# Last 64 channels mixed in four 64x64 tiles, weights asked for later, a wider output ring and a new hand-written order, in a convolution and token-mixing kernel

## The chip, the cores and the metric

The kernel runs on one core of a Trainium2 chip. A core has TensorE (PE in the profile; its weight loads are shown apart as PEld), VectorE (DVE), ScalarE (ACT), GpSimd (POOL) and SyncE (SP), which run their own instruction streams and meet through semaphores, and 16 DMA engines that move data between the chip's main memory and the core's own memory (SBUF). Matmul results land in PSUM, which has 8 banks of 128 partitions x 512 float32 values. The metric is device time in microseconds (us); lower is better. Here it is the median of the runs of one kernel.

## The reference

The input x has shape (8, 4224, 192): 8 batches, 4224 tokens, 192 channels.

1. A causal convolution over 7 tokens. The channels form 8 heads of 24; each head has its own 7 taps, which are a softmax over a row of `weight` (8, 7). `y[s] = sum_k w[h, k] * x[s - 6 + k]`.
2. A linear token mixing with `w_q` and `w_k` (192, 64): `W_tok = (y w_q)(y w_k)^T / 8`, `mixed = W_tok y`, with no softmax.
3. `out = relu(mixed) w_out`, with `w_out` (192, 192).

As step 2 has no softmax, it can be computed as `mixed = (y w_q) (w_k^T (y^T y)) / 8`. The 4224 x 4224 matrix is never formed; what is formed for each batch is the 192 x 192 Gram matrix `G = y^T y` and the 64 x 192 matrix `M = w_k^T G / 8`.

## The kernel before

**Work of one batch.** The tokens stand on 128 partitions in 33 chunks of 128. A batch goes through these kinds of operations (the names are those of the program):

- *load* (POOL's queue): x arrives as bfloat16 in one of `NX` places of `XW`, in two DMAs (batch 0 in four).
- *conv* and *conv_other* (PE, L575): one pair for each head, each four 64x64 matmuls against a banded matrix; two PSUM banks. *y* (ACT or DVE, L607) copies the result to `Y` as bfloat16. Batch 0 is cut into three pieces of chunks, so it has 24 pairs and 24 evacuations.
- *yt* (DVE, L622): four operations that transpose `Y` in 32x32 blocks; *wq* (PE, L640): 48 matmuls of 512 columns in 32x64 tiles give `y w_q` transposed in four banks; *wqt* (L657) evacuates it into `WQT` in two halves, one for tokens 0 to 2047 and one for tokens 2176 to 4223, on partitions 0 to 63 and 64 to 127. The middle chunk has a path of its own (*tr_mid*, *ytl*, *wq_mid*, *wqt_mid*).
- *gram* (PE, L708): six operations that accumulate G; *g*, *turn*, *gt*, *m*, *ms*: G is evacuated, partly transposed, multiplied with w_k and scaled into `MSB` (128 channels) and `MBD` (the last 64 channels, block-diagonal).
- *mix_lo* (PE, L801) and *mix_hi* (PE, L809 or L813): mixed and transposed for 4 x 512 tokens in each half and for the middle chunk; *rt* and *rh* (L827, L828) evacuate them through relu into `RT`. mix_lo covers channels 0 to 127 in two banks, mix_hi the last 64 channels in one bank.
- *fin* and *fin_other* (PE, L859, L876): products with `w_out`; *out* (L894) copies two banks into one of `NOUT` places of `OUT`; *store* (SP's queue, L906; the middle chunk's is L907) writes a place to main memory once both *out* operations that fill it are done. A later *out* that uses the same place waits until that store has landed.

**Order.** `PLAN`, a list written out in the source, gives one order for all 921 operations: an entry is a number, a letter and PSUM banks. The letter chooses the engine (A is ACT, D is DVE, G is POOL, S is SP) or, on PE, the shape of the tiles in which the matmuls are issued: F is the full 128x128 array, C is 128x64 tiles (two at once), R is 64x128 (two at once), Q is 64x64 (four at once), W is 32x64. Each engine executes its own entries strictly in the order of the list; so do the two DMA queues, POOL's with the loads and SP's with the weights and stores. `Program.place` puts in front of each operation the semaphore waits that its inputs, its PSUM banks and its buffers need; a wait holds up everything behind it on the same engine.

**Places of the rings** are in one line: `NX, NYT, NRT, NOUT = 6, 1, 4, 7` (x, transposed y, relu results, outputs).

**Order around the change.** "store 3.1" below is the first store of batch 3 in SP's order, "out 3.9" the ninth *out* of batch 3 in the plan. Decoded from `PLAN`:

- SP's stores, in order: 0.1 0.2 0.3 1.1 0.4 1.2 0.5 1.3 1.4 1.5 2.1 2.2 3.1 3.2 2.3 2.4 2.5 3.3 4.1 3.4 4.2 3.5 and so on. Store 3.1 needs out 3.3 and out 3.5; store 2.3 needs out 2.6 and 2.7; store 2.5 needs out 2.1 and 2.5. Out 3.9 uses the place of store 2.5.
- DVE between *wq* of batch 0 and *wq* of batch 1: wqt, g, y, y, gt, ms, cast, ms, cast, ms, y, yt, rt, yt, yt, rh, yt (and then rt, out, y, out, y).
- PE around *wq* of batch 0: gram (4), wq, gram (2), eight conv pairs of batch 1 with turn and m among them.
- PE's 479 operations change tile shape 128 times. mix_hi for 512 tokens is issued 8 times as F (one matmul) and 24 times as C (two matmuls).

**Start.** The taps become banded matrices through a chain of small DVE, ACT and PE operations; four weights (w_k; w_q in two layouts; w_out) are asked for on SP's queue as soon as the taps' weights have landed, in 12 DMAs. PE executes a few matmuls on zeros (*run_up*) first.

Of the kernel before, what the change touches and what calls it, by code (L numbers as in the profile page):

```python
# [22 lines left out]
119Q 104Q 114D 120A 662G 105D 111A 134C2 138C3 52A 135D 130D 143C 559G 140C 128D 142C 560G 129D 131W64 661G 141C
132A 133D 139C 159Q0 144D 156Q6 160Q 157Q 153Q4 161A 174Q2 158D 175Q 154Q 171Q0 176A 155D 172Q 162Q6 173A 145C2
163Q 146D 168Q4 164A 147C3 165Q0 148D 169Q 53D 166Q 149D 170A 47D 150D 763G 167D 136C2 212R6 137A 201R4 234R2
177D 203A 188C0 764G 235C1 214D 193C 213C4 202C5 190C 204A 178D 192C 237A 189C 236A 179D 224C6 191C 215A 226D
241R2 194A 180D 267Q4 223R6 242R 225D 268Q 243A 208R0 209F 269A 270Q2 210D 255Q6 271Q 256Q 272A 219R4 257D 227R0
220R 228R 221A 261Q2 229D 273Q6 262Q 274Q 263A 216R4 275D 230R0 217R 231R 181W26 232A 218A 195C0 183D 196A 264Q4
182A 197F1 184F0 265Q 198D 276Q6 266D 199A 258Q2 200A 277Q 259Q 278A 304F1 260D 205R4 185A 238R6 306A 206R 303R2
207A 239R 290C0 240D 305A 293C 211S 281D 233S 186C1 245R4 314R6 222S 247A 310R2 316A 187D 325R4 279D 311R 291C  # L30
327A 280D 326C1 315C6 246C7 295C 317A 248D 292C 282D 312A 294C 286C4 328A 249R5 307R6 287D 296A 250R 251D 308R
347R2 366Q0 349D 363Q4 309D 367Q 372Q2 364Q 368A 373Q 365D 313S 357Q6 374A 297C0 252S 337C1 298D 378Q4 339A 358Q
369Q2 379Q 359A 360Q0 380D 361Q 370Q 375Q6 362A 371D 376Q 462Q4 377A 463Q 336R0 464D 283W26 338A 340R4 284A 285D
341F 299F0 342A 321R2 300D 329R6 301D 382D 302A 322R 318R4 343R0 323A 330F 344F 331D 348C2 345A 428F3 319F 350D
332R6 381D 320A 405R0 351R2 333F 407A 352F 439C4 392C5 441D 334A 395C 353D 397C 430D 354S 288C0 406C1 244S 393C
383D 408A 324S 388C4 438R6 389A 335S 427R2 440D 417C1 346S 429A 396C 394C 419A 289D 384D 471Q6 398A 477Q2 472Q
478Q 480Q0 473D 468Q4 479A 481Q 469Q 482D 470A 434R6 416R2 435F 418D 385W40 436A 420R6 387A 386D 412R2 421R 413R
422A 465Q0 414D 474Q4 466Q 475Q 467A 459Q6 476D 570Q2 460Q 571Q 461A 409R0 399F4 410F 400D 572A 483D 401F5 431R6
402A 411A 442R2 403D 432R 404D 443R 433A 445R4 415S 449R0 444D 446F 451A 423R6 447A 529R0 519F2 530F3 531A 424F
532D 508F4 494C5 425A 521D 450C0 497C 486D 452A 426S 510A 576Q2 579Q6 561Q0 577Q 580Q 562Q 578D 581A 498C 496C  # L40
563A 484D 490C4 453R2 518R6 507R0 520D 454R 390C3 499C 491A 495C 455A 509A 541C4 391D 485D 564Q6 573Q2 565Q 574Q
500D 533R0 575A 566D 534F 535A 582Q2 543D 663Q6 583Q 664Q 567Q4 584A 684Q0 665D 568Q 685Q 569A 514R2 686D 522R6
515R 511R4 516A 523R 512R 524D 540R0 513A 596C2 501C3 542A 525R6 502D 551R4 526F 553D 503F3 487W40 504D 505A
527A 506A 528S 547R6 489A 488D 517S 552C3 597C 448S 554A 548R 585D 456S 536R0 549A 544R4 437S 537R 587D 545R
538A 631R6 599C 546D 633A 539S 601C 632C3 492C0 586D 634A 493D 555R1 620R4 609R6 622A 556R 621C3 588D 600C 592C0
611A 598C 557D 593D 610C4 602D 643C5 612D 589W06 645A 623A 774Q4 590A 591D 669Q2 775Q 670Q 671A 642R0 776D 768Q6
644A 603C2 594C3 604D 769Q 595D 681Q4 765Q2 770A 682Q 766Q 683D 638R0 767A 624R6 639R 613R4 640A 625R 614R 649R2
616R0 650R 617R 615A 626D 651A 646R4 618D 635R6 647R 653R2 636R 648D 655A 619S 783Q0 637A 678Q2 550S 784Q 679Q
785A 675Q4 680D 786Q6 676Q 787Q 677A 666Q0 788D 654C2 667Q 656A 605F3 668A 672Q4 606D 771Q6 607D 673Q 772Q 608A
780Q0 674A 773D 777Q2 781Q 778Q 782A 723F4 779D 657R5 627R6 725A 722R0 658R 628R 688D 711R2 659A 629A 734C4  # L50
698C5 689D 724A 630S 699C 558S 687D 712C6 694C7 713A 703C 652S 745C0 700C 714D 641S 695A 701C 690D 747A 702C
736A 744R2 704A 733R6 746D 715R0 735A 729R4 716R 730F 717D 691W26 731D 726R0 693A 692D 740R4 727R 741R 728A
718R6 792D 751R2 742A 732S 748R0 719R 752R 749R 720A 705C4 800C5 706D 750D 753A 696C4 721S 707C6 756C7 802C 708A
758D 697A 754S 790D 709A 755R2 737R0 710A 660S 757A 813R6 759R4 791D 738R 760R 846R2 761A 804C 815A 789D 762S
825C4 801C 848A 739D 814C6 805C 847C7 816A 827D 803C 743S 849A 824R2 806D 820R0 826D 835R6 817R4 837A 821F 818F
822D 850R2 819A 828R6 851R 853R0 823S 852A 829R 807C4 858C5 854R 808A 860D 831R2 830D 855A 809F4 832F 836F5 856S
833A 793W06 838D 810D 834S 811D 812A 842R2 794A 795D 839R4 843R 840R 844A 841D 865R0 866C6 867A 878C7 868D 796C2
845S 877R4 797A 869R0 879A 857R2 870F 859D 880D 873R2 871A 861R6 798C4 874F 799D 872S 862R 901R0 875D 881R4 903A
902F7 882F 904D 876S 890C2 863A 914C3 883D 892A 864S 905R0 889R6 906R 891D 884S 909R4 907A 910F 908S 911A 885R0
916D 913R6 897R2 915D 886R 912S 898R 887A 893R4 917R6 899D 894F 918F 888S 919A 895D 900S 920S 896S  # L60
# [121 lines left out]
def bass_lightweight_conv__then__hypermixer_token_mlp_kernel(  # L182
# [8 lines left out]
    B, S, D = x.shape  # L191
    H, KC = weight.shape
    DH = moe_w_q.shape[1]
# [23 lines left out]
    NX, NYT, NRT, NOUT = 6, 1, 4, 7  # L217
# [242 lines left out]


# [33 lines left out]
    def gen_weight(name, pairs):  # L495
        def emit(e, op):
            return [(e.dma_start(d, s), 16) for d, s in pairs]

        return add(
            "S", emit, needs=[load_w], dma=(name, semaphore(f"s_{name}"), 16 * len(pairs)), kind="weights"  # L500
        )

    def split(t, n, cols):
        return [
            (WLO[:, cols], bass.AP(t, 0, [[n, LO], [1, n]])),
            *((WHI[p : p + HI, cols], bass.AP(t, LO * n, [[n, HI], [1, n]])) for p in (0, HI)),
        ]
# [5 lines left out]
            (WQ6F[32 * i : 32 * i + 32, :, :], bass.AP(wq_t, 0, [[2 * DH, 32], [64 * DH, 3], [1, 2 * DH]]))  # L513
            for i in range(NBLK)
        ],
    )
    load_t = gen_weight("wt", [split(wq_t, DH, QS)[i] for i in (0, 2)])
# [267 lines left out]
    def gen_mix(b, j, evm):  # L785
# [11 lines left out]
        def mix_lo(e, op):  # L797
            last = None
            for i in range(2):
                p = slice(64 * i, 64 * i + DH)  # L800
                last = e.matmul(  # L801
                    bank(op.bank[0] + i)[:, 0:n], MSB[p, mb, :], WQT[p, wqb, q0 : q0 + n], start=True, stop=True
                )
            return last

        def mix_hi(e, op):
            ps = bank(op.bank[0])
            if op.letter == "F":
                return e.matmul(ps[:, 0:n], MBD[:, mb, :], WQT[:, wqb, q0 : q0 + n], start=True, stop=True)  # L809
            last = None  # L810
            for i in range(2):
                to = ps[64 * i : 64 * i + HI, 0:n] if whole else ps[0:HI, n * i : n * i + n]
                last = e.matmul(  # L813
                    to, MBD[:, mb, 64 * i : 64 * i + HI], WQT[:, wqb, q0 : q0 + n],
                    start=whole or i == 0, stop=whole or i == 1, skip_group_check=True,
                )
            return last

        ml = add("R", mix_lo, needs=[*evm, *evq], after=free, banks=(2,), kind="mix_lo", batch=b)
        mh = add("FC" if whole else "C", mix_hi, needs=[*evm, *evq], after=free, banks=(1,), kind="mix_hi", batch=b)  # L820
# [3 lines left out]
        def relu(dst, src):  # L824
# [8 lines left out]
        hi_to = RT[:, slot, 2, 0:n] if whole else RT[0:64, slot, 2, 0 : 2 * n]  # L833
# [4 lines left out]
        )  # L838
        rh = add(
            "AD",  # L840
            relu(hi_to, lambda: bank(mh.bank[0])[:, 0:n] if whole else bank(mh.bank[0])[0:64, 0 : 2 * n]),
            needs=free, drains=(mh, 0), kind="rh", batch=b,
        )

# [147 lines left out]
```

## Time and profile before

| | |
|---|---|
| three timed runs | 169.04, 167.09, 168.16 us; median 168.16 us |
| profiled execution | 168.92 us; span of its instructions 167.2 us |
| mean granted TensorE clock in it | 0.928 of full |
| busy share of the span | PE 86%, DVE 71%, ACT 68%, POOL 13% |
| moved by DMA | read 26.49 MB, written 25.95 MB |

In the page, line 2 of the profile cuts the span into 40 slices of 4.18 us; a digit is the busy share of a slice in tenths, PEclk the granted clock in tenths. "L708 PE" is a group of instructions of source line 708 on PE. In the rows of a wait, "A <- B: 5.5, 1, 5.5" means that A stood idle for 5.5 us in total, once, at longest 5.5 us, until B released it. A row of the timeline is start, duration, engine, line, operation, tiles, shape and count; equal neighbours are merged, and the idle time ahead of a row stands behind it in brackets. A row of the windows has, for each engine, busy us and the number of instructions, then the granted clock, the share of DMA engines at work (over 1 where packets overlap) and GB/s. PE's rows show matmuls with their modelled pipeline, so neighbours overlap.

### The profile page before, as it was taken

The numbers are of one execution on the slowest core, as the hardware profiler recorded it, in microseconds if no ns is written. First come the engines' busy times: TensorE is split into PE (matmuls) and PEld (weight loads), VectorE is DVE, ScalarE is ACT, GpSimd is POOL, SyncE is SP. The second block draws the span as 40 slices with busy tenths as digits, with TensorE's granted clock in tenths as the row PEclk, the third lists the DMA queues.
The fourth block names the chain that finished last, engine by engine and source line by source line (L and its number), as shares of the span: only waits on it lengthen the run. The fifth ranks groups of instructions, "written<-read, shape, count | busy, mean of one in ns | idle before, by whom it ended". The sixth has DMA issues, their size and how long they took to land.

```text
span 167.2 us, 6244 instructions
## 1 busy us (share of the span) xinstructions
PE 143.7 (86%) x2839; PEld 93.8 (56%) x2845; DVE 118.3 (71%) x191; ACT 113.8 (68%) x184; POOL 21.1 (13%) x23
## 2 busy tenths in 40 slices
PE   5837599999999999999999999619999999998960
PEld 1324376376647736765667567403765867874640
DVE  4714294799778877798878959425688897967870
ACT  3135332767689798877996889803999957889760
POOL 7990305050053000000000000000000000000000
PEclk9965557999999999999999999996999999999995
DMA  2999999999999999999999928970045878989897
GB/s 21 173 195 207 191 195 191 193 193 194 193 196 191 299 343 313 195 202 340 337 282 314 227 35 306 386 275 1 4 170 211 298 295 319 381 317 397 320 356 281
DMA packets 46474, 39.86 MB, mean 238 GB/s; under 512 B 35568, under 2 KB 39280, under 8 KB 46448
## 3 DMA queue, kind: packets, MB, share of 16 engines
q0 software_dynamic: 34080, 12.98, 64.9%
q1 hardware_dynamic: 12368, 26.49, 43.9%
q8 instruction: 22, 0.36, 0.8%
q14 instruction: 4, 0.03, 0.0%
HBM read 26.49 MB, written 25.95 MB: 314 GB/s over the span
## 4 chain that ended last, share of the span: by engine, by line
PE 66%; DMA 13%; DVE 9%; ACT 3%; issue 2%; SPq 2%; POOL 2%; DVEq 1%; POOLq 0%
PE ps L575 14%; PE ps L708 14%; PE ps L859 12%; PE ps L876 9%; DMA xw<-in_x_dram 8%; PE ps L640 7%; DMA out_dram<-out_sb 5%; PE ps L801 4%; DVE y L607 3%; PE ps L813 3%; DVE out_sb L894 2%; POOL xw L484 2%; SPq L906 1%; ACT out_sb L894 1%; PE ps L284 1%
## 5 line engine op out<-in xcount | busy, mean ns | idle before, releaser
L575 PE MATMUL ps<-xw,band 64*64 64x384 bf16 (+4 forms) x480 | 36.1, 331 | 6.9 <-DMA xw<-in_x_dram 4.2
L607 ACT CAST y<-ps 128x792 bf16<-128x792 f32 (+3 forms) x49 | 31.3, 666 | 12.9 <-PE ps L575 12.2
L827 ACT ACTIVATE rt<-ps 128x1024 bf16<-128x1024 f32 (+3 forms) x50 | 36.4, 764 | 4.4 <-PE ps L801 2.3
L894 ACT COPY out_sb<-ps 128x768 f32<-128x768 f32 (+1 forms) x46 | 33.9, 749 | 5.9 <-PE ps L876 5.2
L575 PE MATMUL ps<-xw,carry 64*64 64x384 bf16 (+2 forms) x160 | 35.2, 327 | 0.0
L607 DVE CAST y<-ps 128x792 bf16<-128x792 f32 (+3 forms) x31 | 26.1, 859 | 10.1 <-PE ps L575 10.0
L708 PE MATMUL ps<-y 128*64 128x192 bf16 (+2 forms) x792 | 30.1, 228 | 0.2 <-DVE y L607 0.2
L622 DVE STREAM_TRANSPOSE yt<-y 128x768 uint32<-128x768 uint32 x32 | 29.9, 957 | 0.1
L575 PEld LDWEIGHTS ps<-xw,band 64*64 64x64 bf16 x480 | 16.6, 112 | 24.0 <-PE ps L575 7.0
L708 PEld LDWEIGHTS ps<-y 128*64 128x64 bf16 x792 | 27.9, 115 | 3.4 <-issue 1.5
L894 DVE COPY out_sb<-ps 128x768 f32<-128x768 f32 (+1 forms) x26 | 22.7, 881 | 9.8 <-DMA out_dram<-out_sb 5.5
L876 PE MATMUL ps<-wol,rt 64*128 64x192 bf16 (+1 forms) x264 | 25.1, 250 | 0.8 <-issue 0.2
L859 PE MATMUL ps<-woh,rt 64*128 64x192 bf16 x264 | 23.4, 250 | 1.3 <-ACT y L607 0.4
L484 POOL DMA_DIRECT2D xw<-in_x_dram x18 | 20.7, 1166 | 29.9 <-issue 29.2
L828 DVE TENSOR_SCALAR rt<-ps 128x512 bf16<-128x512 f32 (+3 forms) x30 | 20.8, 702 | 4.7 <-PE ps L801 1.7
L640 PE MATMUL ps<-yt,wq 32*64 32x512 bf16 x384 | 14.1, 425 | 5.6 <-DVE ytl L289 5.3
L657 ACT CAST wqt<-ps 128x1024 bf16<-128x1024 f32 x8 | 8.1, 1013 | 15.4 <-PE ps L640 15.4
L876 PEld LDWEIGHTS ps<-wol,rt 64*128 64x128 bf16 (+1 forms) x264 | 15.1, 115 | 6.3 <-PE ps L859 2.2
L657 DVE CAST wqt<-ps 128x1024 bf16<-128x1024 f32 x8 | 9.8, 1225 | 9.6 <-PE ps L640 9.6
L859 PEld LDWEIGHTS ps<-woh,rt 64*128 64x128 bf16 x264 | 11.7, 114 | 8.2 <-issue 2.5
L859 PE MATMUL ps<-wol,rt 64*128 64x192 bf16 x178 | 15.6, 243 | 0.0
L575 PEld LDWEIGHTS ps<-xw,carry 64*64 64x64 bf16 x160 | 15.2, 112 | 0.0
(118 smaller groups left out, 118.4 us busy)
## 6 DMA issues: line engine op xcount, KB each, us to landing
out_dram<-out_sb SPq DMA_DIRECT2D x28, 768.0 KB, 6.9
xw<-in_x_dram POOLq DMA_DIRECT2D x7, 816.0 KB, 31.8
xw<-in_x_dram POOLq DMA_DIRECT2D x7, 768.0 KB, 27.9
out_dram<-out_sb SPq DMA_DIRECT2D x8, 384.0 KB, 3.1
xw<-in_x_dram POOLq DMA_DIRECT2D x3, 384.0 KB, 10.2
out_dram<-out_sb SPq DMA_DIRECT2D x8, 96.0 KB, 5.1
xw<-in_x_dram POOLq DMA_DIRECT2D x1, 432.0 KB, 5.7
wq6f<-in_moe_w_q_dram SPq DMA_DIRECT2D x4, 48.0 KB, 6.0
```

What stands on the lines that cost most here:

```text
L484: lambda e, op, dst=dst, src=src: e.dma_start(dst, src),
L575: lambda p=p, a=a, w=w, back=back: e.matmul(at(op, p, a, z), w, XW[r : r + 64, s, a - back : z - back, g], start=start, stop=not start, sk ...
L607: return e.copy(dst, src) if op.letter == "A" else e.tensor_copy(dst, src)
L622: return e.transpose(dst, src)
L640: last = e.matmul(bank(op.bank[i // 2] + i % 2)[DH * half : DH * half + DH, :], WQ6[p, j, s, :], YT[p, tb, half * NK : half * NK + NK, 64 ...
L657: return e.copy(to, src) if op.letter == "A" else e.tensor_copy(to, src)
L708: mm = e.matmul(at[p : p + 64, o : o + z - r], Y[:, yb, c, r : r + 64], Y[:, yb, c, r:z], start=st, stop=end, skip_group_check=True,)
L827: return e.activation(dst, src(), AF.Relu)
L828: return e.tensor_scalar(dst, src(), 0.0, None, op0=ALU.max)
L859: last = e.matmul(bank(op.bank[0] + a)[:, (i - q) * D : (i - q) * D + D], RT[p, slot, a if lo else 2, i:width:nt], WOL[p, :] if lo else WO ...
L876: last = e.matmul(bank(fh.bank[0] + a)[:, (i - q) * D : (i - q) * D + D], RT[p, slot, a, i:width:nt], WOL[p, :], start=False, stop=True, s ...
L894: return e.copy(dst, src) if op.letter == "A" else e.tensor_copy(dst, src)
```

## The change

- **mix_hi.** For 512 tokens it is four matmuls of 256 columns in 64x64 tiles (letter Q): two for each half, one for tokens 0 and 1 of every four and one for tokens 2 and 3. They write two banks instead of one; the layout of the third part of `RT` and the rows that *fin* takes follow. An *out* now covers all four of every four tokens of one half, not two of every four in both halves. The two stores of a place in the last batch are one for each half, with runs of 3 KB instead of 1.5 KB.
- **mix_lo** may be issued as Q (four matmuls in 64x64 tiles) or R; it is so 11 times of 40.
- **Weights** are in nine DMAs and wait for the first load of x.
- **Rings**: `NX, NYT, NRT, NOUT = 5, 2, 4, 10`.
- **Fillers**: eight new PE operations on zeros, six of one matmul of 512 columns (F) and two of two matmuls (C), that write a PSUM bank nobody reads. Three stand in the convolution of batch 0, one each in batches 3 and 5's convolutions, and three after *fin* 6.6.
- **Order**: a new `PLAN` of 929 entries. Tile shape changes 151 times on PE (487 operations); fin_other is issued 40 times as F and 32 times as R (before: 23 and 49). On PE all six grams of batch 0, its turn, m and tr_mid come ahead of its *wq*, and that ahead of batch 1's convolution. Between *wq* of batch 0 and *wq* of batch 1 PE has twelve conv pairs, four mix_lo and four mix_hi of batch 0, four grams of batch 1, two fins with their fin_others in F, one wq_mid and 8 changes of shape; DVE has ms (3), wqt, a memset, y (5), a cast, rh (2), rt (1) and yt (4), the last entry a yt. SP's stores are: 0.1 1.1 0.2 0.3 0.4 2.1 1.2 0.5 1.3 1.4 2.2 1.5 2.3 2.4 3.1 2.5 3.2 3.3 4.1 3.4 4.2 4.3 4.4 3.5 4.5 5.1 and so on; store 3.2 needs out 3.9 alone, store 3.5 needs out 3.2 and 3.3, out 5.5 and out 5.7 use the place of store 3.5, out 3.9 that of store 1.5.

```diff
 PLAN = """                          # all lines replaced
...
-    NX, NYT, NRT, NOUT = 6, 1, 4, 7
+    NX, NYT, NRT, NOUT = 5, 2, 4, 10
...
+    filler = None
+    for _ in range(8):
+        def fill_up(e, op):
+            out = bank(op.bank[0])
+            if op.letter == "F":
+                return e.matmul(out, RUNUP[:, 0:128], RUNUP[:, :], start=True, stop=True)
+            e.matmul(out[0:64], RUNUP[:, 0:64], RUNUP[:, :], start=True, stop=True)
+            return e.matmul(out[64:128], RUNUP[:, 64:128], RUNUP[:, :], start=True, stop=True)
+        filler = add("CF", fill_up, needs=[zero_r], after=[run_3, filler], banks=(1,), kind="filler")
...
         return add(
-            "S", emit, needs=[load_w], dma=(name, semaphore(f"s_{name}"), 16 * len(pairs)), kind="weights"
+            "S", emit, needs=[load_w, *load[0, 0]],
+            dma=(name, semaphore(f"s_{name}"), 16 * len(pairs)), kind="weights",
         )
...
         return [
             (WLO[:, cols], bass.AP(t, 0, [[n, LO], [1, n]])),
-            *((WHI[p : p + HI, cols], bass.AP(t, LO * n, [[n, HI], [1, n]])) for p in (0, HI)),
+            (WHI[:, cols], bass.AP(t, LO * n, [[0, 2], [n, HI], [1, n]])),
         ]
...
         def mix_lo(e, op):
             last = None
-            for i in range(2):
...
+            cols = (slice(0, LO),) if op.letter == "R" else (slice(0, 64), slice(64, LO))
+            for col in cols:
+                for i in range(2):
+                    p = slice(64 * i, 64 * i + DH)
+                    last = e.matmul(
+                        bank(op.bank[0] + i)[col, 0:n], MSB[p, mb, col], WQT[p, wqb, q0 : q0 + n],
+                        start=True, stop=True, skip_group_check=True,
+                    )
             return last
 
         def mix_hi(e, op):
-            ps = bank(op.bank[0])
-            if op.letter == "F":
-                return e.matmul(ps[:, 0:n], MBD[:, mb, :], WQT[:, wqb, q0 : q0 + n], start=True, stop=True)
...
+            for c in range(2):
+                for i in range(2):
+                    if whole:
+                        p = slice(64 * i, 64 * i + DH)
+                        last = e.matmul(
+                            bank(op.bank[0] + i)[64 * c : 64 * c + HI, 0:256].rearrange("p (g k) -> p g k", k=2),
+                            MBD[p, mb, p],
+                            WQT[p, wqb, q0 : q0 + n].rearrange("p (g k) -> p g k", k=4)[:, :, 2 * c : 2 * c + 2],
+                            start=True, stop=True, skip_group_check=True,
+                        )
...
-        ml = add("R", mix_lo, ..., banks=(2,), ...)
-        mh = add("FC" if whole else "C", mix_hi, ..., banks=(1,), ...)
+        ml = add("RQ", mix_lo, ..., banks=(2,), ...)
+        mh = add("Q" if whole else "C", mix_hi, ..., banks=(2,) if whole else (1,), ...)
...
+        na, ni = (2, 2) if whole else (1, 1)
+        apiece = b == B - 1 and whole
+        for half in range(na):
+            def rows(p, i, lo, half=half):
+                if not whole:
+                    return RT[p, slot, 0 if lo else 2, 0:128]
+                if lo:
+                    return RT[p, slot, half, i:512:4]
+                return RT[p, slot, 2, 256 * half + i % 2 : 256 * half + 256 : 2]
...
```

More of the change, by code (lines that the diff above doesn't have):

```diff
@@ L23 @@
[L23 to L27, printed above, removed]
@@ L61 @@
+906F 912A 806C2 44C3 880S 807D 907D 913R6 917R4 914R 918R 908S 915A 922C3 901R0 919A 916S 921Q6 902F 923D 924A
+920S 903D 925R2 926R 927D 928S 904S
 """.split()
@@ L804, in mix_lo @@
             return last
         def mix_hi(e, op):
-            ps = bank(op.bank[0])
-            if op.letter == "F":
-                return e.matmul(ps[:, 0:n], MBD[:, mb, :], WQT[:, wqb, q0 : q0 + n], start=True, stop=True)
             last = None
[L811 to L816, printed above, removed]
@@ L817, in mix_hi @@
-            return last
-        ml = add("R", mix_lo, needs=[*evm, *evq], after=free, banks=(2,), kind="mix_lo", batch=b)
-        mh = add("FC" if whole else "C", mix_hi, needs=[*evm, *evq], after=free, banks=(1,), kind="mix_hi", batch=b)
+            for c in range(2):
[8 more added lines that the diff above has]
+                        )
+                    elif c == 0:
+                        last = e.matmul(
+                            bank(op.bank[0])[0:HI, n * i : n * i + n],
+                            MBD[:, mb, 64 * i : 64 * i + HI],
+                            WQT[:, wqb, q0 : q0 + n],
+                            start=i == 0, stop=i == 1, skip_group_check=True,
+                        )
@@ L821, in gen_mix @@
+            return last
+        ml = add("RQ", mix_lo, needs=[*evm, *evq], after=free, banks=(2,), kind="mix_lo", batch=b)
+        mh = add("Q" if whole else "C", mix_hi, needs=[*evm, *evq], after=free, banks=(2,) if whole else (1,), kind="mix_hi", batch=b)
         m_read.setdefault(b, []).extend([ml, mh])
@@ L869, in gen_mix, with fin_other @@
             fh = add("R", fin, needs=[rl, rh, *casts_o], after=ofree, banks=(na,), kind="fin", batch=b)
-            def fin_other(e, op, iq=iq, q=q, fh=fh):
+            def fin_other(e, op, rows=rows, fh=fh):
                 last = None
-                for i in iq:
-                    for a in range(na):
-                        p = slice(64 - 64 * a, 128 - 64 * a) if op.letter == "R" else slice(0, 128)
+                for i in range(ni):
+                    for c in range(na):
+                        p = slice(64 - 64 * c, 128 - 64 * c) if op.letter == "R" else slice(0, 128)
                         last = e.matmul(
-                            bank(fh.bank[0] + a)[:, (i - q) * D : (i - q) * D + D],
-                            RT[p, slot, a, i:width:nt],
+                            bank(fh.bank[0] + c)[:, i * D : i * D + D],
+                            rows(p, 2 * c + i, True),
                             WOL[p, :],
```

138 lines of the change are left out of this document (69 added, 69 removed).

## The prediction, on record before the changed kernel ran

> **What bounds the kernel now.** I read the page first, then the sums by stage, the waits and the timeline.
>
> ```profile
> span 167.2 us, 6244 instructions
> ...
> PE   5837599999999999999999999619999999998960
> PEclk9965557999999999999999999996999999999995
> DMA  2999999999999999999999928970045878989897
> GB/s 21 173 195 207 191 195 191 193 193 194 193 196 191 299 343 313 195 202 340 337 282 314 227 35 306 386 275 1 4 170 211 298 295 319 381 317 397 320 356 281
> ```
>
> PE has nines nearly everywhere except at three places: the start (DMA saturated, PE waiting for x, granted clock 0.5), one hole two thirds through the span, and the end. The sums by stage cut at those places and at the wq groups:
>
> ```profile
> 26.04:45.55 19.51, 18.94 (x398) 11.68 (x397) 15.79 (x22) 12.76 (x18) 4.70 (x4) 0.98 1.60 193
> 45.55:107.14 61.59, 59.90 (x1230) 39.40 (x1233) 48.84 (x69) 51.89 (x78) 3.67 (x3) 1.00 1.22 261
> 107.14:112.39 5.25, 0.00 (x1) 0.00 (x1) 0.61 (x3) 1.09 (x2) 0.00 (x0) 0.99 0.86 327
> 112.39:115.25 2.86, 2.86 (x52) 1.11 (x56) 0.81 (x3) 0.00 (x1) 0.00 (x0) 0.50 0.02 6
> 115.25:149.35 34.10, 33.29 (x690) 23.78 (x689) 28.49 (x37) 29.63 (x48) 0.00 (x0) 0.99 0.62 233
> 149.35:161.79 12.44, 11.43 (x181) 7.36 (x182) 9.97 (x16) 9.66 (x14) 0.00 (x0) 1.00 0.97 357
> 161.79:167.20 5.41, 0.01 (x1) 0.00 (x0) 1.03 (x2) 0.32 (x1) 0.00 (x0) 0.65 0.85 299
> ```
>
> From 26 to 107 and from 115 to 149 PE is busy 97% of the time, with DVE and ACT at 79 to 87% from 45 on: PE sets the pace, but evacuation is close behind it. The fourth column (DVE) and the fifth (ACT) say so stage by stage. In the hole, 5.25 us, no engine works and DMA moves 327 GB/s; after it, 2.86 us run at half clock. The waits name it:
>
> ```profile
> PEld ps L640 <- DVE ytl L289: 5.8, 1, 5.8
> DVE out_sb L894 <- DMA out_dram<-out_sb: 5.5, 1, 5.5
> SPq L906 <- ACT mbd L769: 13.2, 1, 13.2
> ```
>
> The timeline around it:
>
> ```profile
> 98.98 1.57 PE L640 MATMUL ps<-yt,wq 32*64 32x512 bf16 x48
> 99.52 0.78 ACT L894 COPY out_sb<-ps 128x768 f32<-128x768 f32 x1
> 100.32 2.41 SPq L906 DMA_DIRECT2D out_dram<-out_sb  x3
> 102.78 1.22 SPq L907 DMA_DIRECT2D out_dram<-out_sb  x1
> 104.05 2.57 SPq L906 DMA_DIRECT2D out_dram<-out_sb  x2
> 111.78 0.36 DVE L894 COPY out_sb<-ps 128x192 f32<-128x192 f32 x1 [5.50 <-DMA out_dram<-out_sb]
> 112.39 2.79 PE L640 MATMUL ps<-yt,wq 32*64 32x512 bf16 x48 [5.29 <-DVE ytl L289]
> ```
>
> SP's head for 13.2 us is store 3.1, which needs out 3.5 (ACT, 99.52 to 100.30). Stores 2.3, 2.4 and 2.5, whose outs were done before, stand behind it. All six leave from 100.32 on, share the DMA engines, and out 3.9, which needs store 2.5's place, holds DVE until 111.78. Behind out 3.9 on DVE stands ytl of batch 5, and PE's next wq waits for DVE.
>
> **The change, part by part.**
>
> *1. The hole.* With ten places out 3.9 reuses store 1.5's place. That store stands before store 2.3 in SP's new order, a batch earlier. So this wait goes: 5.25 us, plus the half clock behind it. The wq takes 2.79 us there against 1.57 us at 98.98: 1.2 us, and the conv behind it loses 0.1 more until 115.25. I take **-6.6 us**. Bounds: -8 (other small waits go with it) to 0 (it comes back elsewhere; the rival below).
>
> *2. mix_hi.* What four 64x64 tiles do at once is seen on conv, which is issued so:
>
> ```profile
> 87.22 0.35 PE L575 MATMUL ps<-xw,carry 64*64 64x384 bf16 x1
> 88.06 0.32 PE L575 MATMUL ps<-xw,carry 64*64 64x384 bf16 x1
> L813 PE MATMUL ps<-wqt,mbd 128*64 128x512 bf16 x48 | 9.4, 386 | 0.0
> ```
>
> Between the two conv rows lie five rounds of four matmuls of 384 or 408 columns: 0.84 / 5 = 0.168 us a round, so 0.42 ns a column whatever the number of tiles. (A round needs this for about 400 columns.) A mix_hi of 512 columns, as C or F, holds PE for 512 x 0.42 = 0.215 us; 386 ns in the row is that and the pipeline. With four tiles of 256 columns it is 0.107 us. 32 of them: **-3.4 us**. The stride of its rows is no new cost: wq reads every second element, and its 6 rounds of 512 columns are 1.29 us of its 1.57, the rest being pipeline. Bounds: -3.4 to 0 (the tiles take turns).
>
> *3. Changes of tile shape.* The letters of the plan change 151 times on PE instead of 128. What one costs:
>
> ```profile
> 94.97 0.34 PE L575 MATMUL ps<-xw,band 64*64 64x384 bf16 x2
> 95.25 0.35 PE L859 MATMUL ps<-woh,rt 64*128 64x192 bf16 x4
> 98.11 0.19 PE L801 MATMUL ps<-wqt,msb 64*128 64x64 bf16 x2
> 98.34 0.52 PE L876 MATMUL ps<-wol,rt 128*128 128x192 bf16 x4
> ```
>
> 384 columns take 0.16 us from 94.97, so PE could go on at 95.13 and does at 95.25: 0.12 us lost. After 64 columns (0.03 us) from 98.11 it goes on at 98.34: 0.20 us lost. I take 0.11 us, the nearer one, since in the second the weights of a full array had to be loaded as well and few changes are of that kind: 23 x 0.11 = **+2.5 us**. Bounds: 0 (they fall into waits) to 23 x 0.20 = +4.6.
>
> The Trainium skill, TensorEngine Tiling (Array Packing), section Tiling Modes, says of this: "Changing tiling mode (not just tile) drains the TensorE". The rows agree with 0.12 and 0.20 us; the page gives no price, so by it the term has the same sign and no other size.
>
> That fin_other is F 40 times instead of 23 costs nothing by itself: 4 matmuls of 192 columns on the whole array stream as long (4 x 0.08) as the 8 half-array ones that they replace, in pairs.
>
> *4. Fillers.* 512 columns, 0.215 us each. The three in batch 0's convolution lie beside waits for x and bands; five are on the path: **+1.1 us** (0 to +1.1).
>
> *5. From the start to wq of batch 1.* Rows of before:
>
> ```profile
> 18.36 0.37 PE L575 MATMUL ps<-xw,band 64*64 64x192 bf16 x1 [2.55 <-DMA xw<-in_x_dram]
> 22.54 3.57 PE L708 MATMUL ps<-y 128*64 128x192 bf16 x63
> 26.04 1.94 PE L640 MATMUL ps<-yt,wq 32*64 32x512 bf16 x48
> 86.05 0.68 PE L708 MATMUL ps<-y 128*64 128x192 bf16 x17
> ```
>
> The last x of batch 0 lands at 18.36, with DMA saturated. The weights come later but are the same half megabyte by the shapes in the source, and still ahead of that piece: 0 (if all of them fell behind it, 0.5 MB at the 195 GB/s of the GB/s line would be -2.5; if they held the matmuls of batch 0's wq or m up, +1). No work stands on SP behind the new wait but the stores from 51 us on. Now six grams at half clock instead of four precede wq: 22.5 + 5 = 27.5. On DVE g stands ahead of the last yt, so wq follows at 27.5 + 0.3 + 1.0 + 0.2 = 29.0 instead of 26.04, with the turn, m, tr_mid and two grams done that came later before (some 2.5 us at their clock): +0.5. Then wq ends at 30.6. Behind it DVE has, ahead of the next wq:
>
> ```profile
> L622 DVE STREAM_TRANSPOSE yt<-y 128x768 uint32<-128x768 uint32 x32 | 29.9, 957 | 0.1
> L607 DVE CAST y<-ps 128x792 bf16<-128x792 f32 x24 | 23.0, 980 | 3.7 <-PE ps L575 3.6
> L657 DVE CAST wqt<-ps 128x1024 bf16<-128x1024 f32 x8 | 9.8, 1225 | 9.6 <-PE ps L640 9.6
> L828 DVE TENSOR_SCALAR rt<-ps 128x1024 bf16<-128x1024 f32 x8 | 9.7, 1214 | 1.0 <-PE ps L801 0.8
> L828 DVE TENSOR_SCALAR rt<-ps 128x512 bf16<-128x512 f32 x13 | 8.8, 680 | 1.6 <-PE ps L809 0.8 <-PE ps L813 0.6 <-PE ps L876 0.2
> ```
>
> 1.23 + 5 x 0.98 + 2 x 0.68 + 1.21 + 4 x 0.96 + 0.3 of small ones = 12.8 us. PE has twelve conv pairs (0.335 each, two rounds), four mix_lo (0.215), four mix_hi (0.107), four grams (0.5, from 17 matmuls in 0.68 with the pipeline), 1.1 of fin and wq_mid and eight changes: 9.3 us. So DVE is what the second wq waits for, at 30.6 + 12.8 + 0.2 = 43.6. That is still earlier than 45.55, but with less of PE's work behind it: PE waits 3.7 us there (14.6 from 29.0, less 1.6 for the wq and 9.3). Before, the same stage of 19.51 us held 16.9 by the same prices: the wq, thirteen conv pairs, eight mixes (0.215 each), six grams of six chunks and two of three, six fins with their fin_others (0.5 each), 0.4 of small ones, twenty changes. It lost 2.6. So +1.1, and with the +0.5 of the chain **+1.6 us** (0 to +4).
>
> *6. Rings and loads.* With five places of x, load 6 waits for batch 1's conv (about 35 us) and loads 5 follow it on POOL's queue; before, they were issued at about that time too. No conv is reached near its landing: 0. A second place of transposed y only takes waits away: 0 (to -1). Two banks for mix_hi: 0, and the slower rival if not.
>
> *7. The end.* After PE's last matmul 5.41 us go to the last outs, stores and landings, at 299 GB/s. Runs of 3 KB instead of 1.5 KB: **-0.3** (0 to -1).
>
> Sum: -6.6 - 3.4 + 2.5 + 1.1 + 1.6 - 0.3 = -5.1 us. The profiled execution took 168.92 us (1.7 of it outside the span) and would take 163.8. It is 0.76 above the median of 168.16, so the median of the changed kernel comes to **163.1 us**.
>
> **Rivals.**
>
> *A. The clock stays up at the start: 160.1 us.* The Trainium skill, TensorE: Matmul & The Clock Gate, Part 1, says that the clock falls after an idle window of about 3.4 us and returns after a busy one, the windows running freely. Here PEclk is at 5 or 6 from the third slice to the sixth, though no idle stretch was as long as a window, so the trace asks for less idleness than that sentence. If the early fillers keep the clock at full, the grams of batch 0 take 2.5 us instead of 5, and the conv behind the last x gains about 0.5: -3.0. Against it: the fillers are 0.2 to 0.4 us each, and the gap ahead of 18.36 alone is 2.55.
>
> *B. The hole comes back: 167.6 us.* SP's new order has the same fault: store 3.2 waits for out 3.9 alone, and 3.3, 4.1, 3.4 and 3.5 stand behind it; 3.5's place is wanted by out 5.5. With 3.5 the burst has six whole stores of 786 KB (by the shape), 2.0 us each at the 386 GB/s of the GB/s line: 12 us and some 2 to land. From out 3.9 to out 5.5 PE has some 16 us of work by the prices of parts 2 to 5. The margin is 2 us; if 4.2, which waits for out 4.9, leaves 6 us late, as store 3.1 did by more, a wait of 4 to 5 us comes back: +4.5.
>
> *C. Slower: 171.1 us.* mix_hi now holds two of eight banks until rh has read them (0.61 to 0.68 us). If each of 32 costs PE a wait of 0.25 us for a free pair, that is +8. It decides from (5.1 + 1.7) / 32 = 0.21 us each. Against it: PE lost only 3% to all waits in the long stages, with six other operations that take pairs.
>
> *D. The four tiles take turns: 166.5 us.* Then part 2 is 0. Against it speak the conv rounds, which are issued in the same way.
>
> **How the numbers follow.** Forecast 0.50 (161 to 166, from parts 3 and 5 at their ends), A 0.18, B 0.14, D 0.07, C 0.11. About 1% (1.7 us) is what a measurement of this kernel tells from no change. Faster: A, nearly all of the forecast, a little of B: 0.69. Same: most of B and D: 0.19. Slower: C and a part of B: 0.12. The range leaves out C and the far side of A, 0.16 in all: 158.5 to 168.8.
>
> **What would show it.** Right: no DVE wait for out_dram of over 1 us, clock 1.0 from about 27 us to the end of PE's work; mix_hi rows of 64x256 with a round every 0.11 us; wq of batch 1 at 43 to 44 us behind a yt; PE's end at 156 to 158. Wrong: a new row "out_sb <- DMA out_dram" of several us (B), PE rows waiting for rh (C), wq of batch 7 later than 146, or a clock at full before 20 us (A).

## The result: slower by 5%, and the profile after

The changed kernel takes 176.81 us (median of four runs, 175.12 to 177.16), the kernel before 168.6 (four runs): ratio 1.048, interval 1.038 to 1.058. The prediction said 163.1 and a range up to 168.8. It was wrong in sign and outside its range. Medians here are of all runs; ratios and intervals leave out a run that is over 1.5% above the fastest of its kernel (one each in experiments 4, 6 and 10).

The page of the profiled execution (176.94 us), the lines that answer to those shown of before:

```profile
span 175.2 us, 6279 instructions
...
PE 146.8 (84%) x2862; PEld 93.4 (53%) x2867; DVE 121.3 (69%) x187; ACT 113.7 (65%) x188; POOL 21.1 (12%) x23
...
PE   5987602198899899799999999999999998999980
...
PEclk9999999999999999999999999999999999999996
DMA  3999999999959999999920099972068998849796
GB/s 28 174 185 199 193 197 192 192 193 193 178 61 185 194 195 249 225 195 332 384 81 9 4 356 392 382 288 98 4 239 326 388 394 337 345 176 390 298 391 267
```

Two of the three places where PE stood before have changed. The hole two thirds through the span is gone. In its place there is a dent in the sixth slice to the eighth (4.38 us each): 0, 2, 1. DMA shows nines there, so the transfers go on while PE stands. The waits name it:

```profile
DVE wkm L290 <- DMA whi<-in_moe_w_k_dram: 12.1, 1, 12.1
...
ACT wq L290 <- DMA wq6f<-in_moe_w_q_dram: 7.9, 1, 7.9
PE ps L723 <- ACT y L622: 7.8, 1, 7.8
...
PE ps L723 <- DVE y L622: 4.3, 1, 4.3
...
DVE out_sb L933 <- DMA out_dram<-out_sb: 1.7, 1, 1.7
```

The fifth row is the one that the change was predicted to take away, and most of it is gone: 1.7 us instead of 5.5. (`wlo` holds the first 128 rows of a weight, `whi` its last 64, twice; `wq6f` is w_q in a layout of its own, four times over. A cast of each to bfloat16 stands on DVE or ACT.) The first two are new. The cast of w_k on DVE (*wkm*) stands for 12.1 us until `whi` has landed, the cast of w_q on ACT (*wq*) 7.9 us until `wq6f` has. Behind them on the same engines stand the evacuations *y* of batch 0's last pieces, and PE's grams wait for those (third and fourth row). The chain that ended last goes through the same place:

```profile
18.28 1.65 SPq L511
19.97 12.50 DMA whi<-in_moe_w_k_dram
34.56 4.56 PE ps L723 x54
```

The sums by stage, cut ahead of the dent (20.39), at the gram that ends it (34.56), at *wq* of batches 0 and 1 and at PE's last matmul (length of the stage; PE, PEld, DVE, ACT, POOL busy; granted clock; DMA share; GB/s):

```profile
20.39:34.56 14.17, 2.03 (x39) 1.47 (x36) 1.85 (x9) 1.47 (x5) 1.17 (x1) 1.00 1.56 194
34.56:40.55 5.99, 5.16 (x91) 4.74 (x91) 3.28 (x6) 0.27 (x1) 0.00 (x0) 1.00 1.60 192
40.55:54.87 14.32, 13.35 (x258) 6.83 (x257) 12.77 (x19) 11.51 (x16) 4.81 (x4) 1.00 1.24 146
...
170.67:175.20 4.53, 0.09 (x1) 0.00 (x0) 0.49 (x2) 0.00 (x0) 0.00 (x0) 0.68 0.70 273
```

In the 14.17 us ahead of 34.56 PE works for 2.03. *wq* of batch 0 starts at 40.55 where 29.0 was predicted; from there on the stages are near the forecast (14.32 us to the next *wq*, 14.6 predicted). So 11.5 us are lost ahead of 40.55, in the dent. Transfers of weights on SP's queue (start of the issue, its length), first of the changed kernel, then of the kernel before:

```profile
7.40 0.67 SPq L511 DMA_DIRECT2D whi<-in_moe_w_out_dram  x1
...
9.59 8.64 SPq L511 DMA_DIRECT2D wq6f<-in_moe_w_q_dram  x3
18.28 1.65 SPq L511 DMA_DIRECT2D wlo<-in_moe_w_k_dram  x1
19.97 1.03 SPq L511 DMA_DIRECT2D whi<-in_moe_w_k_dram  x1
```

```profile
5.32 3.04 SPq L497 DMA_DIRECT2D wq6f<-in_moe_w_q_dram  x4
```

Three `wq6f` take 8.64 us to issue, where four took 3.04. The last issue, of w_k, is done at 21.0, and w_k lands at 32.47: 11.5 us for two transfers of 32 KB. The new order asks for w_k last; in the kernel before it was the first, at 3.70.

### The profile page after: what moved, and what is told of

Read it like the earlier page. It is cut to its first block, busy times and chain, and to the rows that moved or that the text cites. A ratio compares the mean times of both kernels' runs of the same rounds, so it can differ in the third digit from the quotient of the medians.

```text
span 175.2 us, 6279 instructions
## 1 busy us (share of the span) xinstructions
PE 146.8 (84%) x2862; PEld 93.4 (53%) x2867; DVE 121.3 (69%) x187; ACT 113.7 (65%) x188; POOL 21.1 (12%) x23
## 4 chain that ended last, share of the span: by engine, by line
PE 60%; DMA 15%; DVE 9%; SPq 8%; issue 3%; ACT 1%; ACTq 0%; DVEq 0%; POOLq 0%
PE ps L723 12%; PE ps L915 11%; PE ps L898 11%; PE ps L590 10%; SPq L511 7%; DMA whi<-in_moe_w_k_dram 7%; PE ps L655 6%; DMA out_dram<-out_sb 5%; DVE y L622 4%; PE ps L818 4%; DMA xw<-in_x_dram 3%; PE ps L831 2%; DVE out_sb L933 2%; PE ps L278 1%; DVE rt L855 1%
## 5 line engine op out<-in xcount | busy, mean ns | idle before, releaser
L590 PE MATMUL ps<-xw,band 64*64 64x384 bf16 (+4 forms) x480 | 39.3, 332 | 5.8 <-issue 2.0
L723 PE MATMUL ps<-y 128*64 128x192 bf16 (+2 forms) x792 | 29.6, 232 | 12.1 <-ACT y L622 7.8
L590 PE MATMUL ps<-xw,carry 64*64 64x384 bf16 (+2 forms) x160 | 38.1, 327 | 0.0
L854 ACT ACTIVATE rt<-ps 128x1024 bf16<-128x1024 f32 (+3 forms) x49 | 34.7, 732 | 4.8 <-PE ps L818 3.6
L622 DVE CAST y<-ps 128x792 bf16<-128x792 f32 (+3 forms) x34 | 27.2, 816 | 13.1 <-PE ps L590 12.8
L855 DVE TENSOR_SCALAR rt<-ps 128x512 bf16<-128x512 f32 (+3 forms) x31 | 23.6, 769 | 7.2 <-PE ps L818 3.5
L915 PE MATMUL ps<-wol,rt 128*128 128x192 bf16 (+1 forms) x264 | 26.9, 250 | 0.2
L898 PE MATMUL ps<-woh,rt 64*128 64x192 bf16 x264 | 21.7, 246 | 1.1 <-DVE out_sb L933 0.6
L915 PEld LDWEIGHTS ps<-wol,rt 128*128 128x128 bf16 (+1 forms) x264 | 16.8, 115 | 5.5 <-PE ps L898 2.9
L898 PEld LDWEIGHTS ps<-woh,rt 64*128 64x128 bf16 x264 | 9.6, 95 | 9.0 <-issue 2.0
L818 PE MATMUL ps<-wqt,msb 64*128 64x512 bf16 (+3 forms) x102 | 13.2, 354 | 0.6 <-DVE rt L855 0.3
L655 PE MATMUL ps<-yt,wq 32*64 32x512 bf16 x384 | 12.5, 386 | 0.1
```

What stands on the lines that cost most here:

```text
L590: lambda p=p, a=a, w=w, back=back: e.matmul(at(op, p, a, z), w, XW[r : r + 64, s, a - back : z - back, g], start=start, stop=not start, sk ...
L622: return e.copy(dst, src) if op.letter == "A" else e.tensor_copy(dst, src)
L655: last = e.matmul(bank(op.bank[i // 2] + i % 2)[DH * half : DH * half + DH, :], WQ6[p, j, s, :], YT[p, tb, half * NK : half * NK + NK, 64 ...
L723: mm = e.matmul(at[p : p + 64, o : o + z - r], Y[:, yb, c, r : r + 64], Y[:, yb, c, r:z], start=st, stop=end, skip_group_check=True,)
L818: last = e.matmul(bank(op.bank[0] + i)[col, 0:n], MSB[p, mb, col], WQT[p, wqb, q0 : q0 + n], start=True, stop=True, skip_group_check=True,)
L854: return e.activation(dst, src(), AF.Relu)
```

## Experiments

**Theory F** (few): a DMA whose source repeats in its outermost dimension, `[0, 2]` for `whi` and `[0, 4]` for `wq6f`, is carried by few of the 16 DMA engines, and there it takes turns with x. **Theory L** (late): it is the later asking that puts the weights behind x. All runs of the changed kernel below keep its plan, rings and tiles (experiment 7 issues some of its matmuls twice).

**1. The old twelve DMAs, still asked for late.**

```diff
-            (WHI[:, cols], bass.AP(t, LO * n, [[0, 2], [n, HI], [1, n]])),
+            *((WHI[p : p + HI, cols], bass.AP(t, LO * n, [[n, HI], [1, n]])) for p in (0, HI)),
...
-            (WQ6F[:, j, :], bass.AP(wq_t, 64 * DH * j, [[0, NBLK], [2 * DH, 32], [1, 2 * DH]]))
-            for j in range(3)
+            (WQ6F[32 * i : 32 * i + 32, :, :], bass.AP(wq_t, 0, [[2 * DH, 32], [64 * DH, 3], [1, 2 * DH]]))
+            for i in range(NBLK)
...
-    load_t = gen_weight("wt", split(wq_t, DH, QS))
+    load_t = gen_weight("wt", [split(wq_t, DH, QS)[i] for i in (0, 2)])
```

> The changed kernel with the weights asked for in the old twelve DMAs (no source that repeats in its outer dimension), still behind the first load of x. Theory F (a DMA whose source repeats 2 or 4 times in its outer dimension keeps only one or two packets moving at a time beside x's, where the old pieces kept 4 to 8): the last weights land by 19 to 21 us instead of 32.5, no engine waits for them, the first grams start at 23 to 24 us instead of 34.6, and the kernel takes about 165 us (163 to 167). Theory L (asking 3.3 us later puts the weights behind x): w_k still lands at about 32 and the time stays at 175 to 177.

Measured: 165.34 us, ratio to before 0.987 (0.982 to 0.992). That is 11.5 us less than the changed kernel by the medians and 10.3 by the two ratios to before, about what was missing at 40.55. What the queues did is in the DMA view. First the changed kernel from 25 to 32 us, then this one from 11 to 18; q0 carries x, q1 the weights, and the last column is the time of all packets as a share of 16 engines' time:

```profile
DMA packets 3562, 1.35 MB, mean 192 GB/s; under 512 B 3476, under 2 KB 3562, under 8 KB 3562
...
q0 software_dynamic: 3324, 1.27, 150.1%
q1 hardware_dynamic: 238, 0.08, 7.2%
```

```profile
DMA packets 3588, 1.41 MB, mean 201 GB/s; under 512 B 2953, under 2 KB 3587, under 8 KB 3587
...
q0 software_dynamic: 2340, 0.89, 103.8%
q1 hardware_dynamic: 1247, 0.50, 40.4%
```

7.2% of 16 engines is 1.15 packets of the weights in flight; 40.4% is 6.5. In seven microseconds 238 packets of the weights moved in the one (34 a microsecond) and 1247 in the other (178), beside a DMA that was full in both. On SP's queue and on DVE of this run:

```profile
9.99 2.02 SPq L511 DMA_DIRECT2D wq6f<-in_moe_w_q_dram  x4
...
12.53 1.11 SPq L511 DMA_DIRECT2D whi<-in_moe_w_k_dram  x2
```

```profile
21.74 0.97 DVE L637 STREAM_TRANSPOSE yt<-y 128x768 uint32<-128x768 uint32 x1
22.74 0.22 DVE L290 CAST wkm<-wlo 64x128 bf16<-64x128 f32 x1
```

The last weight is issued by 13.6, and the cast of w_k at 22.74 follows the transpose ahead of it without a wait. By L the time would have stayed at 175 to 177; it is 10 us less.

**2. The nine DMAs, asked for early.** `needs=[load_w]` instead of `[load_w, *load[0, 0]]`, nothing else.

> The changed kernel with its nine DMAs asked for early again (SP waits for the taps' weights only, from 3.7 us, not for the first load of x). Theory F: everything that SP issues is 3.3 us earlier and as slow as it is, so w_k lands at about 29 and the kernel takes 173 us (171 to 175). Theory L: w_k lands by 20 and the time is about 165.

Measured: 173.26 us (1.034, 1.027 to 1.041): 3.5 us less by the medians, 2.4 by the ratios, about the 3.3 us by which SP starts earlier, and nothing more. That is what F expects; by L it would have been about 165.

**3. Nine DMAs in the kernel before.** The diff of experiment 1, the other way round, in the old kernel.

> The kernel before with the nine DMAs in place of its twelve, nothing else. SP keeps its old order, w_k first, then the w_q of the six-chunk layout, the other w_q, w_out. Theory F: one or two packets of the weights move at a time from the start, the wq6f piece lands at 16 to 20 instead of 13, the casts of w_q's second layout and of w_out wait until 22 to 30 us, and the kernel is 3 to 10 us slower (171 to 178). Theory L: the form does nothing by itself, 168.5.

Measured: 177.0 us (1.056, 1.050 to 1.063). This edit alone makes the old kernel as slow as the changed one, 9.6 us over its 167.4 in the same session. DVE now waits at three casts, where before it waited 3.0 us at the first alone (brackets: idle time and what ended it):

```profile
13.51 0.22 DVE L289 CAST wkt<-wlo 64x128 bf16<-64x128 f32 x1 [4.96 <-DMA whi<-in_moe_w_k_dram]
...
19.83 0.36 DVE L289 CAST wq<-wq6f 128x384 bf16<-128x384 f32 x1 [3.86 <-DMA wq6f<-in_moe_w_q_dram]
...
29.58 0.26 DVE L289 CAST woh<-whi 128x192 bf16<-128x192 f32 x1 [4.67 <-DMA whi<-in_moe_w_out_dram]
```

Here w_k is asked for first, as of old, and w_out last. So the loss doesn't hang on which weight stands last on SP's queue.

**4. Both undone.** Twelve DMAs, asked for early.

> The changed kernel with both undone: twelve DMAs, asked for from 3.7 us. Both theories: the weights land by 16 to 17 us, the first grams start at 23 to 24 and the time is about 165 (163 to 167). By F it is within 1 us of the kernel with the old form alone, by L it is 10 us below that one. A time above 170 here would say that neither is the cause, and that the rest of the sum (the hole, the mixes, the tile shapes) failed instead.

Measured: 164.42 us (0.980, 0.972 to 0.987). It is 0.9 us below experiment 1 by the medians and 1.2 by the ratios, with intervals that overlap: that is all the later asking could be worth. Its sums by stage, cut at *wq* 0, 1 and 7 and at PE's last matmul:

```profile
28.75:43.08 14.33, 13.36 (x257) 6.83 (x256) 12.77 (x19) 11.52 (x16) 3.67 (x3) 1.00 1.60 193
...
144.24:157.82 13.58, 12.69 (x207) 7.42 (x207) 9.49 (x15) 10.32 (x17) 0.00 (x0) 1.00 0.95 367
```

**5 and 6. Is it the repeat, or the size of the outer dimension?** On experiment 1, first with the repeat for `whi` alone:

```diff
-            *((WHI[p : p + HI, cols], bass.AP(t, LO * n, [[n, HI], [1, n]])) for p in (0, HI)),
+            (WHI[:, cols], bass.AP(t, LO * n, [[0, 2], [n, HI], [1, n]])),
...
-    load_t = gen_weight("wt", [split(wq_t, DH, QS)[i] for i in (0, 2)])
+    load_t = gen_weight("wt", split(wq_t, DH, QS))
```

> The changed kernel with the old form of the four wq6f pieces, but the three whi transfers as one DMA each that repeats its 64 rows twice (source [0,2],[n,64],[1,n]); asked for late. Theory F: the 128 packets of w_out's whi go at the 26 a microsecond seen in the changed kernel, those of w_q and w_k at 34, in all 12.4 us from about 11 us on, so w_k lands at 23 to 25 instead of 18.5, with one or two weights' packets moving; 166.5 to 168.5 us. If the wq6f form alone did the harm: lands by 19, 165.3.

then with two DMAs as of old, whose 64 rows are described as two blocks (the second starts one row early, so the last rows of the weights are the wrong ones):

```diff
-            *((WHI[p : p + HI, cols], bass.AP(t, LO * n, [[n, HI], [1, n]])) for p in (0, HI)),
+            *((WHI[p : p + HI, cols], bass.AP(t, LO * n, [[31 * n, 2], [n, 32], [1, n]])) for p in (0, HI)),
```

> As the changed kernel with the old form (165.3 us), each whi still in two DMAs of 64 partitions, but with a source of two times 32 rows whose blocks lie 31 rows apart (source [31n,2],[n,32],[1,n]), so that an outer dimension of 2 stays and nothing is repeated but one row; the last rows of the weights are the wrong ones for that. Theory K (the size of the outermost dimension sets how many DMA engines carry a DMA, 2 here): as slow as the repeat, 1 to 2.5 weights' packets moving at a time in long stretches, w_k lands at 23 to 25, 166.5 to 168.5 us. Theory R (reading the same rows twice is what is slow): w_k lands by 19, 165.3 us.

Measured: 171.1 us (1.023, 1.016 to 1.029) and 168.51 (1.007, 1.003 to 1.010), against 165.34 without either. The weights' queue from 22 to 27 us of the first, from 19 to 25 of the second, and what DVE's cast waited in each:

```profile
q1 hardware_dynamic: 174, 0.05, 6.9%
```

```profile
q1 hardware_dynamic: 206, 0.06, 6.9%
```

```profile
DVE wkm L290 <- DMA whi<-in_moe_w_k_dram: 7.3, 1, 7.3
```

```profile
DVE wkm L290 <- DMA whi<-in_moe_w_k_dram: 5.5, 1, 5.5
```

Both move 34 to 35 packets a microsecond, 6.9% of 16 engines, 1.1 in flight. In the second no DMA reads more than one row twice. So theory K of the expectation holds: an outermost dimension of 2 is what is slow, not the repeat. (The first is 2.6 us over the expected 166.5 to 168.5: there SP needs 5.75 us to issue the four `wq6f` behind it, and w_k lands at 27.5. It also moves 64 packets more than the second, the second copy of w_q's last rows; at 34 a microsecond that is 1.9 us, an estimate that fits the difference of the two waits.) The Trainium skill, DMA: Bandwidth & Descriptors, Rules for kernel authors, has this rule: "an outermost dim of size c < 16 — e.g. a leading zero-stride broadcast of c copies — confines the whole DMA to at most c engines". The runs agree as far as they can show it: 1.1 packets in flight with an outer 2, against 6.5 with outer 64, 128 and 32. Which engines carried them no run here shows, so the "few engines" of F is argued; that the outer 2 of `whi` is what costs the time is shown. Between the first of the two and the changed kernel stands the outer 4 of `wq6f` alone, worth 4.3 us by the ratios (1.048 against 1.023); there repeat and outer dimension were not taken apart.

**7. The four-tile mix, twice.** Experiment 1 with each whole mix_hi issued twice into the same places.

```diff
-            for c in range(2):
+            for c in (0, 1, 0, 1) if whole else (0,):
```

> The changed kernel with the old form (165.3 us), each of the 32 whole mix_hi issued twice into the same places, so one suspected cost is doubled. If the four tiles run at once (0.107 us a round): +3.4 us, 168.7 (167.5 to 169.5). If they take turns (four times 256 columns at 0.42 ns, 0.43 us): +13.7, 179. If PE has slack there: 165.3 to 166.

Measured: 167.47 us (1.002, 0.999 to 1.005), 2.1 above experiment 1 by the medians, 2.4 by the ratios. The groups of mix_hi's line, first of experiment 1, then of this one (mean ns of a matmul last before the bar):

```profile
L831 PE MATMUL ps<-wqt,mbd 64*64 64x256 bf16 x128 | 9.0, 288 | 0.7 <-DVE y L622 0.5 <-ACT rt L854 0.2
```

```profile
L831 PE MATMUL ps<-wqt,mbd 64*64 64x256 bf16 x256 | 12.8, 284 | 2.3 <-issue 1.6 <-DVE y L622 0.5
```

Twice the matmuls for 2.1 to 2.4 us is 0.07 us for each of 32: far from the 0.43 of tiles that take turns, and two thirds of the 0.107 of four at once. PE's busy time for the group says the same: it grows by 3.8 us (9.0 to 12.8), 0.12 for each of 32. The rest would lie beside waits.

**8. Fillers of 16 columns** on experiment 4.

```diff
-                return e.matmul(out, RUNUP[:, 0:128], RUNUP[:, :], start=True, stop=True)
+                return e.matmul(out[:, 0:16], RUNUP[:, 0:128], RUNUP[:, 0:16], start=True, stop=True)
```

(and so for the two halves of form C)

> The changed kernel with the old form asked for early (164.4 us, granted clock 0.98 to 0.99 of the whole span), each of the eight fillers of 16 columns instead of 512. By the sum of the prediction (five of them on the path, 0.215 us each): 163.3 us. If the fillers are what kept the clock at full between 10 and 27 us: the clock falls to 0.93 or 0.94 of the whole span as in the kernel before, the grams of batch 0 take twice as long, and the time is 165.5 to 167.5.

Measured: 163.46 us (0.977, 0.973 to 0.982): 1.0 less than experiment 4 by the medians, 0.4 by the ratios, whose intervals overlap, so a gain is not shown. The clock did not fall:

```profile
PEclk9999999999999999999999999999999999999997
```

**9 and 10. The ring alone, and the changed kernel mended.** In the kernel before, `NX, NYT, NRT, NOUT = 6, 1, 4, 10`; beside it experiment 8 once more.

> The kernel before with ten output places in place of seven and nothing else: part 1 of the change alone. By the sum of the prediction the wait of 5.5 us on DVE for a store's landing goes, with the half clock behind it: 6.6 us less, about 160.8 us (159.5 to 162). If the hole comes back at a later ring place or the engines were late for other reasons behind it: 164 to 167, and a new wait of several us for out_dram shows.

> The changed kernel with the old form of the weights' DMAs, asked for early, and fillers of 16 columns, again on this chip beside the kernel before with ten places, to tell which is faster: 163.5 us as measured already. If the ring is worth what the prediction says, the kernel before with ten places is 2 to 3 us faster than this; if not, this one is the faster by 1 to 3 us.

Measured: 160.79 us (0.962, 0.959 to 0.965) and 163.02 (0.973, 0.969 to 0.977). The old kernel with ten places, one number changed, is the fastest of all, and DVE waits for no store in it. The sums by stage, cut at *wq* 0, *wq* 1, *wq* 7 and PE's last matmul; first the old kernel with ten places:

```profile
0.00:23.91 23.91, 18.23 (x305) 11.03 (x305) 12.72 (x42) 8.44 (x24) 12.75 (x16) 1.00 1.30 163
23.91:43.00 19.09, 18.52 (x390) 11.56 (x388) 15.78 (x22) 12.76 (x18) 4.70 (x4) 1.00 1.61 193
43.00:140.55 97.55, 94.99 (x1970) 64.29 (x1974) 78.67 (x110) 82.47 (x128) 3.67 (x3) 1.00 1.08 269
140.55:152.98 12.43, 11.44 (x181) 7.38 (x182) 10.00 (x16) 9.69 (x14) 0.00 (x0) 1.00 0.95 352
152.98:158.80 5.82, 0.00 (x1) 0.00 (x0) 1.03 (x2) 0.32 (x1) 0.00 (x0) 0.84 0.83 289
```

then the changed one, mended:

```profile
0.00:27.97 27.97, 20.91 (x347) 12.66 (x347) 13.74 (x43) 8.79 (x24) 13.92 (x17) 1.00 1.34 167
27.97:42.30 14.33, 13.36 (x259) 6.84 (x257) 12.78 (x19) 11.52 (x16) 3.66 (x3) 1.00 1.60 193
42.30:143.18 100.88, 98.56 (x2061) 65.75 (x2059) 85.12 (x112) 82.96 (x132) 3.54 (x3) 1.00 1.04 261
143.18:156.73 13.55, 12.40 (x207) 7.34 (x207) 9.30 (x15) 10.33 (x17) 0.00 (x0) 1.00 0.95 369
156.73:161.10 4.37, 0.02 (x1) 0.00 (x0) 0.41 (x2) 0.00 (x0) 0.00 (x0) 0.72 0.64 248
```

## Why the prediction was wrong, by its own steps

**The step that failed is the sentence of part 5 on the weights**: they "are the same half megabyte", therefore "0". Its bytes are right; the rate that it took, the 195 GB/s of the GB/s line, is that of all 16 engines. It costed the time of asking and not the shape of the nine sources, although the rows of before show the old shapes only. It did allow +1 us if the weights held batch 0's *wq* or m up: the right direction, and a tenth of the size. What the runs showed in its place is 10 to 11.5 us (experiment 1), and 9.6 in the old kernel (experiment 3). The same step also looked for what stands behind the new wait on SP alone. The queues that mattered were DVE's and ACT's, where the casts of the weights stand ahead of evacuations for which PE waits.

None of the four rivals was this one. A and B have nothing to do with it, and C, the slower one, put its 8 us at the mixes, ahead of which PE waited 0.7 us in all (row of L831 above). Of "what would show it", the clock from 27 us and the 64x256 rows of mix_hi came out right, the store wait nearly (1.7 us, not under 1), and *wq* of batch 1 at 54.87 instead of 43 to 44 pointed at the stretch ahead of it.

With the weights' DMAs as they were and asked for early, the times of the forecast stand. Experiment 4 has *wq* of batch 0 at 28.75 (29.0), of batch 1 at 43.08 (43.6), PE's last matmul ending at 157.8 (156 to 158), and its profiled execution takes 163.66 us (163.8). Its median, 164.42, is 3.0 below that of before in the same session, not 5.1 (3.4 by the ratio). That the profiled time meets 163.8 is luck: it is the second lowest of four runs, and while part 1 came out whole, the other parts, +1.5 in the sum, come to +3.2 to 3.6. The terms one by one:

- *Part 1, the hole, -6.6:* 167.38 to 160.79 is -6.6. Right, and measured alone. The gain lies where it was said: from *wq* 1 to *wq* 7 it takes 97.55 us, and the four stages of the prediction from 45.55 to 149.35 take 103.80.
- *Part 2, mix_hi, -3.4:* not undone alone. Doubling it cost 2.1 to 2.4: the tiles do run at once (rival D is out), but a third of a round's price did not reach the end. What was saved against the old form no run shows.
- *Part 3, tile shapes, +2.5:* no run isolates it.
- *Part 4, fillers, +1.1:* 0.4 to 1.0 from experiment 8, within its bounds of 0 to 1.1 and not clear of 0.
- *Part 5, the rest of it, +1.6, with parts 2, 3, 6:* the last two profiles have a full clock nearly to the end and the old DMAs for the weights. From *wq* 0 to PE's last matmul the old kernel with ten places needs 19.09 + 97.55 + 12.43 = 129.07 us, the mended one 14.33 + 100.88 + 13.55 = 128.76. The sum had 2.3 less there (-3.4 + 2.5 + 1.1, and 2.5 of work done earlier), the profiles 0.3. Ahead of it *wq* 0 comes 4.06 us later (27.97 against 23.91), where the sum had 3.0. So the new order and tiles together lose 2.2 us (163.02 against 160.79), which the sum put at 0.4 (-3.4 + 2.5 + 1.6 - 0.3). Which of mixes, shapes and order is short, these runs don't settle.
- *Part 6:* no matmul after batch 0 waited for x in the mended kernel, though POOL's loads stood for the conv as said.
- *Part 7, the end, -0.3:* 4.53 us against 5.41 behind PE's last matmul, -0.9, and 4.37 against 5.82 in the last two profiles, -1.4. Mis-sized, at or beyond its bound of -1.

*Rival A*, the clock at the start, came true in part and was not worth its 3.0 us. It, and the "half clock" of part 5, took the clock for what makes batch 0's grams slow. The row of before at 22.54, 3.57 us for 63 matmuls, is at a granted clock of 0.50; the same 63 in experiment 9, at 1.00 (row 0.00:23.91 above), are no faster:

```profile
20.45 3.52 PE L708 MATMUL ps<-y 128*64 128x192 bf16 x63
```

The *wq* behind them does follow the clock, 1.94 us in the one and 1.56 in the other. So the 5 us of part 5 for six grams is a right size with a wrong cause; what sets it stays open. And in experiment 9 three runs with a mean clock of 0.994 took 160.63 to 160.81 us, three with 0.952 to 0.958 took 160.50 to 161.41.

*Rival B* is the 1.7 us wait; it is there and small.

## What to carry to other kernels

Cost a DMA by the shape that its descriptors have, not by its bytes or by the number of DMAs: merging copies behind a small outer dimension made "fewer DMAs" five times slower here, 34 packets a microsecond against 178, beside a transfer that filled the engines. A wait added on one queue is priced at every in-order engine that uses what arrives, by what stands behind that use. And when a change has many parts, run the one with the largest predicted share by itself: here one number gave 6.6 us, and all the rest together lost 2.2 even with the old DMAs put back.

## What was not expected of the hardware

- Beside a full DMA, an outermost dimension of 2 left 34 packets a microsecond (256 bytes each where it carried w_k), 1.1 in flight; SP's issue of the DMAs behind it slowed too, from 2.0 us for four `wq6f` in experiment 1 to 5.75 in experiment 5.
- In the changed kernel the granted clock is 1.00 in a stretch of 14.17 us in which PE is busy for 2.03 and idle for 7.8 at a time. In the kernel before, with shorter idle stretches, it is 0.5 to 0.6 at the start. Shortening the fillers left it up in eight of ten runs, and experiment 9, with no fillers at all, had it up in three of six. What lowers it here stays open. That the time hardly shows it fits the grams of batch 0, which took 3.52 us at 1.00 and 3.57 at 0.50.
